# Attention and MLP on one core: the first batch's attention in an order of its own, transposes in the MLP's banks, the norm one pair further ahead, and weights rounded in three stages

## Chip, core and metric

The kernel runs on one core of a Trainium2 chip. The metric is the device time of one execution in microseconds (us); less is better. TensorE (PE) multiplies matrices into PSUM, which has eight banks here; VectorE (DVE), ScalarE (ACT) and GpSimd (POOL) do the element work; SyncE (SP) issues the loads and stores. Each engine takes its instructions strictly in the order in which they were written, and an instruction that waits holds up all behind it on its engine.

## Reference

```python
# q, k, v: (batch 8, heads 12, seq 448, dim 64) float32; g_q, g_k: (64)
q_n = q / sqrt(mean(q*q, -1) + 1e-6) * g_q           # and k_n from k, g_k
scores = (q_n @ k_n.T) / sqrt(64)
attn = exp(scores - max(scores)); attn = attn / (sum(attn) + 1e-9)
x = (attn @ v)                                        # to (3584 tokens, 768)
h = x @ w_in                                          # w_in (768, 2048), float64 in memory
g = h - tanh(h)
out = g @ w_out                                       # w_out (2048, 768), float64 in memory
```

## The kernel before

**Work and tiles.** Two heads make a pair; 8 batches of 6 pairs are 48 steps `s`. The 448 rows of a pair are four chunks of 112. With the inputs given, `bounded_path` is taken, which needs no maximum. Per step: `load` brings q, k and v (`q_nat`, `k_nat`, `v_nat`); `norm` squares k and q on POOL (into a tile named `n`), sums on VectorE and raises to -0.5 on POOL (`rr`); `norm_q` multiplies q by its factor on VectorE (tile `n`); `turn` transposes k and normed q on TensorE (L229, L234) and copies them out on ScalarE (`kT`, `qT`); `scores(s, half)` makes the transposed scores of two chunks (four matmuls, L251) and their exponentials on ScalarE (L256), with k's factor as the scale, into a tile `p`; `values` multiplies `p` by v (L280, bank `av`) and by ones for the totals (L289, bank `dn`), and VectorE takes the reciprocal (L294) and the product (L296, `xT`). From the second batch on, `add` first sums the four chunks of `p` on VectorE, so that the totals need two matmuls instead of eight.

**MLP.** For each batch `hidden` makes h by 16 blocks of six matmuls (L313), tanh on ScalarE (L319) and the subtraction on VectorE (L320, `gT`); `project` multiplies by w_out (L353). Batch b's MLP is a generator that `run(gap)` advances between the pieces of the attention of batch b+1, a quarter of a slot at a time.

**Order.** The program is scheduled by hand: what the functions issue, in the order of their calls, is what each engine runs. `slot(s)` is the loop body: it loads pair s+3, norms s+2, scores s+1, and finishes s. In the slots before the MLP starts (s below 6, the first batch) the gaps round weights instead of advancing the MLP.

**Weights.** The float64 weights are read as words and rounded to float32 in 64 pieces of 128x384, numbered n: 32 halves of w_in, then 16 first halves of w_out, then 16 second halves. Piece n is loaded as raw words (w_in's into the tiles that w_out gets later; w_out's into three buffers `w_raw`), then `round_weight_a` (two ScalarE passes, L72 and L73, and a clamp on POOL, L74) and, one piece later, `round_weight_b` (two VectorE passes, L81 and L84, and an add on POOL, L87). `weight(to)` does this up to piece `to` and issues loads up to 14 pieces ahead, 3 ahead for w_out. 20 pieces are done in the first batch, 28 in the blocks of `hidden(0)`, 16 in the first half of `project(0)`.

**Buffers that matter here.** PSUM: four banks `sc`, for scores and transposes; one each for `av` and `dn`; two `mm` for the MLP. SBUF: three tiles `p` (two per step), one `qT` and one `kT`, one `n`, three `rr`, two each of `k_nat` and `q_nat`, three of `v_nat`, three output tiles.

## Time and profile before

| | |
|---|---|
| three runs | 1686.97, 1688.23, 1689.44 us; median 1688.23 |
| profiled execution: its time, its span | 1688.23 us, 1686.4 us |
| busy, of the span: TensorE, VectorE, ScalarE, POOL | 96%, 37%, 24%, 25% |
| TensorE's granted clock, mean | 0.981 |
| slots 1 to 5, each | 16.3 to 17.4 us |
| slots 6 to 10, each | 34.2 to 43.2 us |
| slot 11 | 32.6 us |

A slot s is counted from the first score matmul of `scores(s+1, 0)` on TensorE to the next slot's. The profile's rows give an engine, a line of the code, the operation, out<-in by the names in the program, and times in us (means of one in ns); "idle before <-X" is how long the engine had nothing to run before such instructions, and what ended it. PEclk is the granted clock of TensorE, 1.00 (or 9 in a tenths row) at full speed. One matmul in float32 shows as two records, so x8 is four matmuls. SPq, ACTq and the like are an engine's issue of DMAs and its waits.

### The profile page before, as it was taken

How to read it: one execution, taken by the hardware profiler on the slowest of the kernel's cores; microseconds unless marked ns; L12 is line 12 of the kernel's file. 1: busy time of each engine (PE TensorE's matmuls, PEld its weight loads, DVE VectorE, ACT ScalarE, POOL GpSimd, SP SyncE). 2: the span in 40 equal slices, each digit the busy share in tenths (PEclk: the TensorE clock that was granted, in tenths of full speed). 3: DMA queues.
4: the chain of work that ended last, by engine and by line, in shares of the span. 5: the costliest groups of instructions: out<-in, count | busy, mean ns of one | idle time of the engine just before them, and what ended most of it. 6: DMA issues, size and time to landing. Idle time of an engine off the chain costs nothing.

```text
span 1686.4 us, 14244 instructions
## 1 busy us (share of the span) xinstructions
PE 1615.3 (96%) x5512; PEld 798.6 (47%) x5512; DVE 616.1 (37%) x747; ACT 405.3 (24%) x765; POOL 415.4 (25%) x286
## 2 busy tenths in 40 slices
...
PEclk9788999899999999999999999999999999999999
...
DMA packets 93585, 70.22 MB, mean 42 GB/s; under 512 B 48453, under 2 KB 89413, under 8 KB 93509
## 3 DMA queue, kind: packets, MB, share of 16 engines
...
## 4 chain that ended last, share of the span: by engine, by line
PE 85%; POOL 6%; DVE 4%; issue 3%; DMA 1%; ACT 1%; SPq 0%; ACTq 0%; POOLq 0%; DVEq 0%
PE mm L353 33%; PE mm L313 31%; PE sc L251 9%; PE av L280 8%; PE dn L289 3%; POOL w_out L74 2%; DVE rd L294 2%; POOL w_out L87 1%; PE sc L234 1%; POOL n L205 1%; DMA w_raw<-in_moe_w_out_dram 1%; PE sc L229 1%; POOL rr L209 1%; POOL w_in L87 1%; POOL w_in L74 1%
## 5 line engine op out<-in xcount | busy, mean ns | idle before, releaser
L313 PE MATMUL mm<-xT,w_in 128*128 128x448 f32 x1536 | 601.7, 545 | 7.7 <-DVE gT L320 6.0
L353 PE MATMUL mm<-w_out,gT 128*128 128x384 f32 x1536 | 519.9, 494 | 6.6 <-POOL w_out L87 6.6
L313 PEld LDWEIGHTS mm<-xT,w_in 128*128 128x128 f32 x1536 | 285.7, 190 | 307.5 <-issue 293.6
L353 PEld LDWEIGHTS mm<-w_out,gT 128*128 128x128 f32 x1536 | 287.7, 191 | 233.3 <-issue 38.7
L256 ACT ACTIVATE p<-sc,rr 112x448 f32<-112x448 f32 x384 | 213.0, 635 | 413.8 <-PE sc L251 413.8
L294 DVE RECIPROCAL rd<-dn 128x448 f32<-128x448 f32 x48 | 141.9, 2957 | 308.3 <-PE dn L289 308.3
L205 POOL TENSOR_TENSOR n<-k_nat 112x512 f32<-112x512 f32 x48 | 49.9, 1040 | 736.1 <-PE sc L234 729.2
L251 PE MATMUL sc<-qT,kT 64*112 64x448 f32 x768 | 182.7, 598 | 9.9 <-ACT qT L238 9.9
L320 DVE TENSOR_TENSOR gT<-mm,th 128x448 f32<-128x448 f32 x128 | 79.6, 622 | 289.1 <-ACT th L319 289.1
L319 ACT ACTIVATE th<-mm 128x448 f32<-128x448 f32 x128 | 69.7, 544 | 456.8 <-PE mm L313 447.3
L280 PE MATMUL av<-p,v_nat 112*64 112x448 f32 x768 | 157.6, 553 | 0.0
L209 POOL TENSOR_TENSOR rr<-rr,neg_half 112x16 f32<-112x16 f32 x48 | 139.8, 2913 | 50.6 <-DVE rr L208 49.6
L270 DVE TENSOR_TENSOR sum<-p 112x896 f32<-112x896 f32 x84 | 93.9, 1118 | 124.5 <-ACT p L256 120.1
L251 PEld LDWEIGHTS sc<-qT,kT 64*112 64x112 f32 x768 | 65.2, 183 | 108.4 <-issue 91.4
L206 DVE TENSOR_REDUCE rr<-n 112x8 f32<-112x512 f32 x96 | 65.6, 684 | 138.3 <-POOL n L205 138.3
L280 PEld LDWEIGHTS av<-p,v_nat 112*64 112x64 f32 x768 | 51.7, 139 | 101.8 <-issue 100.7
L353 PE MATMUL mm<-w_out,g_rest 128*128 128x384 f32 x256 | 85.4, 489 | 0.0
L205 POOL TENSOR_TENSOR n<-q_nat 112x512 f32<-112x512 f32 x48 | 50.0, 1041 | 139.1 <-DVE rr L206 139.1
L363 DVE COPY o_sb<-mm 128x384 f32<-128x384 f32 x28 | 15.5, 554 | 153.2 <-PE mm L353 152.9
L353 PEld LDWEIGHTS mm<-w_out,g_rest 128*128 128x128 f32 x256 | 47.9, 190 | 35.6 <-issue 4.1
L333 POOL COPY g_rest<-gT 128x1024 f32<-128x1024 f32 x8 | 9.0, 1131 | 202.2 <-DVE gT L320 202.1
L361 ACT COPY o_sb<-mm 128x384 f32<-128x384 f32 x28 | 13.4, 478 | 188.2 <-PE mm L353 188.1
...
## 6 DMA issues: line engine op xcount, KB each, us to landing
w_out<-in_moe_w_in_dram SPq DMA_DIRECT2D x32, 384.0 KB, 6.8
w_raw<-in_moe_w_out_dram SPq DMA_DIRECT2D x32, 384.0 KB, 3.1
...
q_nat<-in_q_dram SPq DMA_DIRECT2D x48, 224.0 KB, 3.1
v_nat<-in_v_dram SPq DMA_DIRECT2D x48, 224.0 KB, 2.6
...
gcol<-in_g_q_dram ACTq DMA_DIRECT2D x2, 0.2 KB, 2.3
```

Of the source, the lines that this page charges most:

```text
L205: nc.gpsimd.tensor_tensor(out=sq, in0=rows, in1=rows, op=ALU.mult)
L206: nc.vector.reduce_sum(rr[:, i], sq, axis=AX.X)
L209: nc.gpsimd.tensor_tensor(out=rr2, in0=rr2, in1=neg_half, op=ALU.pow)
L251: nc.tensor.matmul(sc[:CP, :S], lhsT=kT[r, c * CP : (c + 1) * CP], rhs=qT[r, :], start=True, stop=True)
L256: nc.scalar.activation(p[:, h, i, :], tiles[h][:CP, :S], AF.Exp, scale=rr[:, 0, 2 * c + h : 2 * c + h + 1])
L270: nc.vector.tensor_tensor(out=u, in0=a, in1=z, op=ALU.add)
L280: nc.tensor.matmul(av[h * D : (h + 1) * D, :S], lhsT=v_nat[:, h, c, :], rhs=p[:, h, c % 2, :], start=(c == 0), stop=(c == NCH - 1),)
L294: nc.vector.reciprocal(rd, dn[:, :S])
L313: nc.tensor.matmul(hps[:, :S], lhsT=w_in_sb[f][:, c, :], rhs=xT[b, c], start=(c == 0), stop=(c == CD - 1))
L319: nc.scalar.activation(th, hps[:, :S], AF.Tanh, bias=0.0, scale=1.0)
L320: nc.vector.tensor_tensor(out=g[:, f, :], in0=hps[:, :S], in1=th, op=ALU.subtract)
L353: nc.tensor.matmul(ops[:, :HALF], lhsT=lhs[:, f, :], rhs=w_out_sb[f][:, d], start=(f == 0), stop=(f == CF - 1),)
```

## The change

1. The first batch gets its own loop body, `first_slot(s)`, from s = -3. Its order on TensorE is scores of s+1 (first half), the transposes of s+2, values of s, scores of s+1 (second half), totals of s. `values` is split into `values`, `totals` and `divide`.
2. In `first_slot` the transposes go into the MLP's two banks `mm`; in later slots into `sc` as before. `qT` and `kT` get two buffers, output tiles two instead of three.
3. `norm` and `norm_q` run for s+3 instead of s+2; k and q are loaded for s+4, v for s+2. The squares get a tile `sq` of their own. In later slots `norm(s+3)` stands ahead of `divide(s)`, and `norm_q(s+3)` behind `turn(s+2)`.
4. A weight is rounded in three stages: a, two ScalarE passes; b, clamp and two passes on VectorE; c, the add on POOL. The clamp leaves POOL. For w_out, c of a piece is issued in the round of the next piece.
5. The first eight pieces of w_out (n = 32 to 39) are loaded into the upper w_out tiles instead of `w_raw`, and loads run up to 14 ahead wherever `place_free` finds the place free by the adds already issued.
6. `add` sums `p` with three adds of 112x896 instead of two of 112x896 and two of 112x448.

The same slot of the first batch on TensorE, before:

```order
L251 MATMUL sc<-qT,kT 112x448 x4
L280 MATMUL av<-p,v_nat 64x448 x8
L289 MATMUL dn<-p,ones 64x448 x8
L251 MATMUL sc<-qT,kT 112x448 x4
L229 MATMUL sc<-ident,k_nat 128x112 x4
L234 MATMUL sc<-ident,n 128x112 x4
```

and now (L271 is the scores, L249 and L254 the transposes, L298 values, L310 totals):

```order
L271 MATMUL sc<-qT,kT 112x448 x4
L249 MATMUL mm<-ident,k_nat 128x112 x4
L254 MATMUL mm<-ident,n 128x112 x4
L298 MATMUL av<-p,v_nat 64x448 x8
L271 MATMUL sc<-qT,kT 112x448 x4
L310 MATMUL dn<-p,ones 64x448 x8
```

The transposes moved from the slot's end to behind its first scores, and the totals from behind the values to the end.

VectorE in such a slot, before, from one reciprocal to the next (w_in_137 is the tile of a block of w_in, w_out_158 a tile of w_out that holds raw words for the time being):

```order
L294 RECIPROCAL rd<-dn 128x448
L296 TENSOR_TENSOR xT<-av,rd 128x4x112
L81 TENSOR_SCALAR w_in_137<-w_in_137 128x384
L84 SCALAR_TENSOR_TENSOR w_in_137<-w_out_158,w_in_137 128x384
L216 TENSOR_TENSOR n<-q_nat,rr 112x2x4x64
L81 TENSOR_SCALAR w_in_138<-w_in_138 128x384
L84 SCALAR_TENSOR_TENSOR w_in_138<-w_out_159,w_in_138 128x384
L206 TENSOR_REDUCE rr<-n 112x8 x2
L208 TENSOR_SCALAR rr<-rr 112x16
```

and now (L78 is the clamp, L235 norm_q, L225 and L227 the norm):

```order
L319 RECIPROCAL rd<-dn 128x448
L321 TENSOR_TENSOR xT<-av,rd 128x4x112
L78 TENSOR_SCALAR w_in_137<-w_in_137 128x384
L79 TENSOR_SCALAR w_in_137<-w_in_137 128x384
L82 SCALAR_TENSOR_TENSOR w_in_137<-w_out_157,w_in_137 128x384
L225 TENSOR_REDUCE rr<-sq 112x8 x2
L227 TENSOR_SCALAR rr<-rr 112x16
L78 TENSOR_SCALAR w_in_137<-w_in_137 128x384
L79 TENSOR_SCALAR w_in_137<-w_in_137 128x384
L82 SCALAR_TENSOR_TENSOR w_in_137<-w_out_158,w_in_137 128x384
L235 TENSOR_TENSOR n<-q_nat,rr 112x2x4x64
```

The norm of a pair and its norm_q, which lay on both sides of a reciprocal, now both stand between two reciprocals, and a clamp heads each weight.

POOL in `project(0)`, where second halves of w_out are rounded, before:

```order
L74 TENSOR_SCALAR w_out_150<-w_out_150 128x384
L87 TENSOR_TENSOR w_out_149<-w_out_149,w_raw 128x384
L74 TENSOR_SCALAR w_out_151<-w_out_151 128x384
L87 TENSOR_TENSOR w_out_150<-w_out_150,w_raw 128x384
L74 TENSOR_SCALAR w_out_152<-w_out_152 128x384
```

and now:

```order
L90 TENSOR_TENSOR w_out_151<-w_out_151,w_raw 128x384
L90 TENSOR_TENSOR w_out_152<-w_out_152,w_raw 128x384
L90 TENSOR_TENSOR w_out_153<-w_out_153,w_raw 128x384
L90 TENSOR_TENSOR w_out_154<-w_out_154,w_raw 128x384
L90 TENSOR_TENSOR w_out_155<-w_out_155,w_raw 128x384
```

The clamps between the adds are gone.

```diff
@@ -67,24 +67,27 @@
 def round_weight_a(nc, raw, dst):
     lo, hi = raw[:, :, 0], raw[:, :, 1]
     nc.scalar.activation(dst, hi.bitcast(F32), AF.Abs, scale=2.0**-16)
     nc.scalar.mul(lo, lo.bitcast(U32), 2.0**-29)
-    nc.gpsimd.tensor_scalar(out=dst, in0=dst, scalar1=HI_MIN, scalar2=HI_MAX, op0=ALU.max, op1=ALU.min)
 def round_weight_b(nc, raw, dst):
-    lo, hi = raw[:, :, 0], raw[:, :, 1]
     bits = dst.bitcast(I32)
+    nc.vector.tensor_scalar(out=dst, in0=dst, scalar1=HI_MIN, scalar2=HI_MAX, op0=ALU.max, op1=ALU.min)
     nc.vector.tensor_scalar(
         out=bits, in0=bits, scalar1=4, scalar2=1, op0=ALU.logical_shift_left, op1=ALU.logical_shift_right
     )
     nc.vector.scalar_tensor_tensor(
-        out=bits, in0=hi, scalar=-(2**31), in1=bits, op0=ALU.bitwise_and, op1=ALU.bitwise_or
-    )
-    nc.gpsimd.tensor_tensor(out=bits, in0=bits, in1=lo, op=ALU.add)
+        out=bits, in0=raw[:, :, 1], scalar=-(2**31), in1=bits, op0=ALU.bitwise_and, op1=ALU.bitwise_or
+    )
+def round_weight_c(nc, raw, dst):
+    bits = dst.bitcast(I32)
+    nc.gpsimd.tensor_tensor(out=bits, in0=bits, in1=raw[:, :, 0], op=ALU.add)
 def bounded_path(tc, ctx, q, k, v, moe_w_in, moe_w_out, out, g_col, ident, ones, neg_half):
@@ -115,12 +118,12 @@
     weights = pool("weights", bufs=1)
     nat = pool("nat", bufs=2)
     small = pool("small", bufs=2)
-    qkp = pool("qkp", bufs=1)
+    qkp = pool("qkp", bufs=2)
     pp = pool("pp", bufs=3)
     sp = pool("sp", bufs=1)
     xp = pool("xp", bufs=9)
     gp = pool("gp", bufs=1)
-    op = pool("op", bufs=3)
+    op = pool("op", bufs=2)
     wp_stack = ctx.enter_context(ExitStack())
     wp = wp_stack.enter_context(tc.tile_pool(name="wp", bufs=3))
     ps_s = pool("ps_s", bufs=4, space=PSUM)
@@ -163,35 +166,51 @@
     def weight_load(n):
         f, i, _ = weight_dst(n)
+        if n < 2 * CF + CF // 2:
+            raw = w_out_sb[n % CF if n < 2 * CF else CF // 2 + f].bitcast(I32).rearrange("p (f w) -> p f w", w=2)
+        else:
+            raw = wp.tile([P, HALF, 2], I32, name="w_raw")
         if n < 2 * CF:
-            raw = w_out_sb[n % CF].bitcast(I32).rearrange("p (f w) -> p f w", w=2)
             rows = w_in_words[i * HALF : (i + 1) * HALF, f * 2 * P : (f + 1) * 2 * P]
             nc.sync.dma_start(
                 out=raw.rearrange("p (c f) w -> p c (f w)", c=CD // 2),
                 in_=rows.rearrange("(c p) f -> p c f", p=P),
             )
         else:
-            raw = wp.tile([P, HALF, 2], I32, name="w_raw")
             nc.sync.dma_start(
                 out=raw.rearrange("p f w -> p (f w)"),
                 in_=w_out_words[f * P : (f + 1) * P, 2 * i * HALF : 2 * (i + 1) * HALF],
             )
         raws[n] = raw
-    done = [0, 0]
+    done = [0, 0, 0]
+    def place_free(n):
+        if n < CF or 0 <= n - 2 * CF - CF // 2 < 3:
+            return True
+        return n - (CF if n < 2 * CF else CF // 2 if n < 2 * CF + CF // 2 else 3) < done[2]
     def weight(to):
-        for n in range(done[1], min(to, 4 * CF)):
+        while done[1] < min(to, 4 * CF):
+            n = done[1]
             round_weight_a(nc, raws[n], weight_dst(n)[2])
             if n:
-                round_weight_b(nc, raws.pop(n - 1), weight_dst(n - 1)[2])
+                round_weight_b(nc, raws[n - 1], weight_dst(n - 1)[2])
             done[1] = n + 1
-            while done[0] < min(max(min(n + 14, 2 * CF + 3), n + 3), 4 * CF):
+            finish_weights(n - 1 if n < 2 * CF else n)
+            while done[0] < min(n + CF - 2, 4 * CF) and place_free(done[0]):
                 weight_load(done[0])
                 done[0] += 1
-        if done[1] == 4 * CF and raws:
-            round_weight_b(nc, raws.pop(4 * CF - 1), weight_dst(4 * CF - 1)[2])
+        if done[1] == 4 * CF > done[2]:
+            round_weight_b(nc, raws[4 * CF - 1], weight_dst(4 * CF - 1)[2])
+            finish_weights(4 * CF)
+    def finish_weights(to):
+        while done[2] < to:
+            round_weight_c(nc, raws.pop(done[2]), weight_dst(done[2])[2])
+            done[2] += 1
     normed, turned, probs, sums, xT = {}, {}, {}, {}, {}
@@ -201,7 +220,7 @@
         rr = small.tile([CP, 2, 2 * NCH], F32, name="rr", bufs=3)
         for i, name in enumerate("kq"):
             rows = loaded[name, s].rearrange("p a b d -> p (a b) d")
-            sq = nat.tile([CP, 2 * NCH, D], F32, name="n", bufs=1)
+            sq = nat.tile([CP, 2 * NCH, D], F32, name="sq", bufs=1)
             nc.gpsimd.tensor_tensor(out=sq, in0=rows, in1=rows, op=ALU.mult)
             nc.vector.reduce_sum(rr[:, i], sq, axis=AX.X)
         rr2 = rr.rearrange("p i r -> p (i r)")
@@ -220,16 +239,17 @@
         )
         normed[s] = rr, n
-    def turn(s):
+    def turn(s, psum):
         rr, n = normed.pop(s)
+        ps, tag = psum
         kn = loaded.pop(("k", s))
-        tk = ps_s.tile([P, 512], F32, name="sc")
+        tk = ps.tile([P, 512], F32, name=tag)
         for c in range(NCH):
             nc.tensor.transpose(tk[:, c * CP : (c + 1) * CP], kn[:, c].rearrange("p h d -> p (h d)"), ident[:CP, :CP])
         kT = qkp.tile([P, S], F32, name="kT")
         nc.scalar.mul(kT, tk[:, :S], g_col)
-        tq = ps_s.tile([P, 512], F32, name="sc")
+        tq = ps.tile([P, 512], F32, name=tag)
         for c in range(NCH):
             nc.tensor.transpose(
                 tq[:, c * CP : (c + 1) * CP], n[:, c].rearrange("p h d -> p (h d)"), ident[:CP, :CP]
@@ -264,14 +284,12 @@
             return
         t = sp.tile([CP, 2, S], F32, name="sum")
         sums[s] = [t]
-        for h in range(2):
-            a, z = (probs[s, half][:, h].rearrange("p c q -> p (c q)") for half in range(2))
-            u = sp.tile([CP, 2 * S], F32, name="sum2")
-            nc.vector.tensor_tensor(out=u, in0=a, in1=z, op=ALU.add)
-            nc.vector.tensor_tensor(out=t[:, h, :], in0=u[:, :S], in1=u[:, S:], op=ALU.add)
+        parts = [probs[s, c // 2][:, :, c % 2, :] for c in range(NCH)]
+        nc.vector.tensor_tensor(out=t, in0=parts[0], in1=parts[1], op=ALU.add)
+        for part in parts[2:]:
+            nc.vector.tensor_tensor(out=t, in0=t, in1=part, op=ALU.add)
     def values(s):
-        b, hp = steps[s]
         v_nat = loaded.pop(("v", s))
         av = ps_v.tile([P, 512], F32, name="av")
         for c in range(NCH):
@@ -281,6 +299,9 @@
                     av[h * D : (h + 1) * D, :S], lhsT=v_nat[:, h, c, :], rhs=p[:, h, c % 2, :],
                     start=(c == 0), stop=(c == NCH - 1),
                 )
+        return av
+    def totals(s):
         dn = ps_v.tile([P, 512], F32, name="dn")
         t = sums.pop(s)
         parts = t if t else [probs[s, c // 2][:, :, c % 2, :] for c in range(NCH)]
@@ -290,6 +311,10 @@
                     dn[h * D : (h + 1) * D, :S], lhsT=ones[:CP, :D], rhs=p[:, h, :],
                     start=(i == 0), stop=(i == len(parts) - 1),
                 )
+        return dn
+    def divide(s, av, dn):
+        b, hp = steps[s]
         rd = sp.tile([P, S], F32, name="rd")
         nc.vector.reciprocal(rd, dn[:, :S])
         x = xT[b, hp] = xp.tile([P, S], F32, name="xT")
@@ -389,40 +414,67 @@
     per_slot = (4 * S / ENGINE_NS * CF * CD + 4 * HALF / ENGINE_NS * CF * 7) / NP
-    def slot(s, gap):
-        def has(i):
-            return 0 <= s + i < NS
-        if has(3):
-            load(s + 3, "kq")
-        if has(2):
-            norm(s + 2)
-        if has(1):
+    def has(s):
+        return 0 <= s < NS
+    def first_slot(s):
+        if has(s + 1):
             scores(s + 1, 0)
-        gap(0)
-        if has(0):
-            values(s)
-        if has(3):
-            load(s + 3, "v")
-        gap(1)
-        if has(2):
-            norm_q(s + 2)
-        if has(1):
+        if has(s + 2):
+            turn(s + 2, (ps_m, "mm"))
+        load(s + 4, "kq")
+        if has(s + 3):
+            norm(s + 3)
+        ahead = 3 * (s + 4) if s < 0 else 9 + (EARLY - 9) * (s + 1) // NP
+        weight(ahead - 2)
+        if has(s):
+            av = values(s)
+        if has(s + 2):
+            load(s + 2, "v")
+        weight(ahead - 1)
+        if has(s + 1):
             scores(s + 1, 1)
             add(s + 1)
-        gap(2)
-        if has(2):
-            turn(s + 2)
-        gap(3)
-    load(0, "kqv")
+        if has(s):
+            dn = totals(s)
+        if has(s + 3):
+            norm_q(s + 3)
+        if has(s):
+            divide(s, av, dn)
+        weight(ahead)
+    def slot(s):
+        gap = per_slot / 4
+        if has(s + 1):
+            scores(s + 1, 0)
+        if has(s + 2):
+            load(s + 2, "v")
+        run(gap)
+        if has(s + 3):
+            norm(s + 3)
+        divide(s, values(s), totals(s))
+        run(gap)
+        if has(s + 1):
+            scores(s + 1, 1)
+            add(s + 1)
+        run(gap)
+        if has(s + 2):
+            turn(s + 2, (ps_s, "sc"))
+        if has(s + 3):
+            norm_q(s + 3)
+        if has(s + 4):
+            load(s + 4, "kq")
+        run(gap)
+    load(0, "kq")
     for n in range(4):
         weight_load(n)
     done[0] = 4
-    for s in range(-2, NP):
-        slot(s, lambda j: weight(EARLY * (4 * (s + 2) + j + 1) // (4 * (NP + 2))))
+    for s in range(-3, NP):
+        first_slot(s)
     for s in range(NP, NS):
-        slot(s, lambda j: run(per_slot / 4))
+        slot(s)
     run(1e9)
```

## Prediction

> **What bounds the kernel now.** I read the page's busy shares first, then its 40 slices.
>
> ```profile
> span 1686.4 us, 14244 instructions
> PE 1615.3 (96%) x5512; PEld 798.6 (47%) x5512; DVE 616.1 (37%) x747; ACT 405.3 (24%) x765; POOL 415.4 (25%) x286
> PEclk9788999899999999999999999999999999999999
> ```
>
> TensorE sets the time, but it is short of work or of clock only in the first eight slices (42 us each). Next, busy time by stage; a stretch here is one slot, from one `scores(s+1, 0)` to the next, and its first number is its length.
>
> ```profile
> 47.14:63.40 16.26, 12.95 (x56) 5.03 (x56) 8.95 (x12) 8.23 (x17) 12.44 (x9) 0.81 0.37 109
> 131.32:171.16 39.84, 37.17 (x109) 16.63 (x109) 28.82 (x38) 17.05 (x36) 30.53 (x23) 0.90 0.13 39
> 171.16:205.34 34.18, 32.79 (x109) 15.26 (x108) 24.21 (x32) 14.87 (x32) 27.28 (x20) 1.00 0.14 41
> 205.34:244.68 39.34, 33.57 (x109) 15.03 (x109) 26.30 (x35) 16.62 (x34) 28.82 (x23) 1.00 0.38 108
> 244.68:287.90 43.22, 35.59 (x122) 18.34 (x121) 26.23 (x33) 16.92 (x34) 32.24 (x24) 0.96 0.43 120
> 287.90:330.47 42.57, 37.19 (x119) 18.27 (x119) 25.20 (x30) 12.95 (x26) 30.80 (x24) 0.88 0.34 99
> 330.47:363.10 32.63, 32.63 (x115) 16.41 (x114) 10.24 (x12) 6.47 (x12) 2.19 (x2) 1.00 0.11 34
> ```
>
> From 330 us on TensorE is busy throughout at full clock and a slot takes 32.63. Slots 6 to 10 (second to sixth row) take 199.15 together, 36.0 more than five such slots: that is the second place with something to win. The first is the first batch, slots 0 to 5, whose TensorE rows are these (start, length, idle before and who ended it):
>
> ```profile
> 47.14 3.33 PE L251 MATMUL sc<-qT,kT 64*112 64x448 f32 x8 [0.68 <-ACT qT L238]
> 50.41 3.44 PE L280 MATMUL av<-p,v_nat 112*64 112x448 f32 x16
> 53.68 3.17 PE L289 MATMUL dn<-p,ones 112*64 112x448 f32 x16
> 56.78 1.76 PE L251 MATMUL sc<-qT,kT 64*112 64x448 f32 x8
> 58.51 0.60 PE L229 MATMUL sc<-ident,k_nat 112*128 112x112 f32 x4
> 61.75 0.98 PE L234 MATMUL sc<-ident,n 112*128 112x112 f32 x4 [2.63 <-DVE n L216]
> 63.40 3.33 PE L251 MATMUL sc<-qT,kT 64*112 64x448 f32 x8 [0.68 <-ACT qT L238]
> ...
> 205.34 1.76 PE L251 MATMUL sc<-qT,kT 64*112 64x448 f32 x8 [1.39 <-ACT qT L238]
> ```
>
> Each slot TensorE waits 2.6 us for the normed q, then 0.7 for the copy of its transpose; the eight score matmuls behind these waits take 3.33 us, against 1.76 inside a run. An idle of 1.39 alone, at 205.34 and amid long runs of matmuls, does not slow them. At full clock the slot's work is 1.76 + 3.2 + 3.1 + 1.76 + about 1.0 of transposes = 10.8. Slots 1 to 5 take 131.32 - 47.14 = 84.2, so 16.84 each.
>
> In slots 6 to 10 the chain is longer; the waits of 120 to 345 us begin with
>
> ```profile
> ACT w_out L72 <- DMA w_raw<-in_moe_w_out_dram: 72.8, 25, 8.0
> ```
>
> ScalarE, which also makes the exponentials and tanh, stands in order behind loads that land late.
>
> **The change, part by part.** Prices first: the groups of VectorE, POOL and ScalarE between 47.14 and 129 us, inside the first batch (busy us, mean ns of one, idle before).
>
> ```profile
> L294 DVE RECIPROCAL rd<-dn 128x448 f32<-128x448 f32 x5 | 14.8, 2958 | 13.7 <-PE dn L289 13.7
> L84 DVE SCALAR_TENSOR_TENSOR w_in<-w_out,w_in 128x384 int32<-128x384 int32 x11 | 9.5, 862 | 0.4
> L206 DVE TENSOR_REDUCE rr<-n 112x8 f32<-112x512 f32 x10 | 6.9, 686 | 25.2 <-POOL n L205 25.2
> L296 DVE TENSOR_TENSOR xT<-av,rd 128x448 f32<-128x448 f32 x5 | 4.8, 962 | 0.2
> L216 DVE TENSOR_TENSOR n<-q_nat,rr 112x512 f32<-112x512 f32 x5 | 4.1, 815 | 0.0
> L81 DVE TENSOR_SCALAR w_in<-w_in 128x384 int32<-128x384 int32 x11 | 3.9, 351 | 0.0
> L208 DVE TENSOR_SCALAR rr<-rr 112x16 f32<-112x16 f32 x5 | 0.9, 175 | 0.2
> ```
>
> ```profile
> L74 POOL TENSOR_SCALAR w_in<-w_in 128x384 f32<-128x384 f32 x13 | 19.7, 1518 | 8.3 <-ACT w_in L72 7.1 <-DMA q_nat<-in_q_dram 1.1
> L209 POOL TENSOR_TENSOR rr<-rr,neg_half 112x16 f32<-112x16 f32 x5 | 14.7, 2946 | 5.0 <-DVE rr L208 5.0
> L87 POOL TENSOR_TENSOR w_in<-w_in,w_out 128x384 int32<-128x384 int32 x12 | 13.5, 1124 | 8.4 <-DVE w_in L84 8.4
> L205 POOL TENSOR_TENSOR n<-q_nat 112x512 f32<-112x512 f32 x5 | 5.2, 1041 | 4.0 <-DVE rr L206 4.0
> ```
>
> ```profile
> L256 ACT ACTIVATE p<-sc,rr 112x448 f32<-112x448 f32 x40 | 22.7, 633 | 34.7 <-PE sc L251 34.7
> L73 ACT ACTIVATE w_out<-w_out 128x384 int32<-128x384 uint32 x13 | 7.2, 556 | 0.0
> L72 ACT ACTIVATE w_in<-w_out 128x384 f32<-128x384 f32 x13 | 7.2, 555 | 0.0
> ```
>
> *Start, to slot 1.* In the new order `turn(2)` stands ahead of `values(0)` and everything else of slot 0, and it needs the loads of pair 2, which still queue behind the first weights. The issue of that load of q, and q's median time to landing in the first 60 us:
>
> ```profile
> 27.25 1.34 SPq L144 DMA_DIRECT2D q_nat<-in_q_dram  x1
> ```
>
> ```profile
> q_nat<-in_q_dram SPq DMA_DIRECT2D x5, 224.0 KB, 7.8
> ```
>
> It lands about 27.25 + 7.8 = 35.0; one weight load more and two loads of v fewer go ahead of it, so I take 34.5. POOL has no clamps left in the way: square 1.04, reduction 0.69, 0.18, power 2.95, norm 0.82 and some handovers: the transposes start near 40.5. Behind them stand 1.0 of slow transposes, `values(0)` (3.2, about 1.2 more at the low clock), 1.7 and 3.1: slot 1 starts at 51.0, 3.9 LATER than the 47.14 of before.
>
> *Slots 1 to 5.* The chain on n is now a slot ahead, so its wait goes. What is late next: `p` has three buffers, and `scores(s+1, 1)` fills the one that `totals(s)` still reads, so its four exponentials start only when `totals(s)` ends, and the next scores need their banks. (Behind them on ScalarE stand one weight's two passes and the next four exponentials, which have time until 7.7 us into the slot.) Four exponentials in a row take 2.2 to 2.5, the second pair of scores 0.9 behind them; with latencies 3.5 until the scores end; then transposes 1.0, values 3.2, scores 1.7, totals 3.1: 12.5. VectorE and POOL have a loop too, since `divide(s)` stands ahead of the reductions of `norm(s+4)` and these ahead of `divide(s+1)`: 2.96 + 0.96 + one weight (clamp 0.35, L81 0.35, L84 0.86) + 0.69 + 1.04 + 0.69 + 0.18 + 2.95 + 0.82, and eight handovers at 0.1: 12.65. I take 12.9 a slot: 5 x 12.9 = 64.5 against 84.2, minus 19.7. Bounds: 12.5 from TensorE, 15.0 if the clock stays as low as now (10.8 / 0.81 + 1.7 idle). Slot 6 then starts at 115.5, minus 15.8. Idle gaps shrink to about 1.5, and the row at 205.34 says that such a gap keeps the clock. The transposes' new banks are the MLP's, which is idle until slot 6: nothing; without that cover they would queue for a bank behind four exponentials, 2.2 us. On SP's queue k and q of s+4 now wait for `turn(s+2)`, with v and weights behind them; all are due a slot or more later and land in some 3 to 8 us: nothing.
>
> *Weights.* Per weight POOL loses 1.52. VectorE gains a clamp whose price no row shows; the nearest is L81, the same form on the same shape, whose later half reads (min/median/max)
>
> ```profile
> L81 DVE TENSOR_SCALAR w_out<-w_out x32: 343/1010/1165, 191.1 to 316.4; 128x384 int32<-128x384 int32 x32
> ```
>
> 0.35 to 1.16; I take 0.5, since POOL, whose rows the long ones meet, gets emptier. In slots 6 to 10, 44 weights are rounded: POOL, 149.7 busy there, falls by 67; VectorE, 130.8, rises by 22 (51 at most) and stays below five slots of 32.63 in the mean. The second halves of w_out go through three `w_raw` buffers: median landing, and the adds of eleven such weights.
>
> ```profile
> w_raw<-in_moe_w_out_dram SPq DMA_DIRECT2D x32, 384.0 KB, 3.1
> ```
>
> ```profile
> L87 POOL TENSOR_TENSOR w_out<-w_out,w_raw x11: 1001/1012/1059, 263.1 to 297.8; 128x384 int32<-128x384 int32 x11
> ```
>
> Ten steps in 34.7, or 3.47 a weight, because POOL held the add of n behind the clamp of n+1, and so behind that one's load. Now add n waits for n alone: 0.4 issue + 3.1 + 1.1 on ScalarE + 1.7 on VectorE (0.5 + 0.4 + 0.8) + 1.0 + 0.7 of handovers = 8.0 for three weights, 2.65 each. `project(0)` rounds one in three matmuls: by columns its 48 are 0.214 of a batch's six slots, 42 us for 16 weights, or 2.6. With a norm that holds POOL some 7 us (1.04 + 0.8 + 1.04 + 1.0 + 2.95) in each slot I get 3.3, and 11 us of lag at the end; 8 of them, a quarter slot, lie between scores and who needs their banks. Loads into w_out's upper tiles are many weights ahead and cost nothing. I leave 12 of the 36.0 lost (1 of it in slot 6, where `sum` and norm_q now stand ahead of the last `divide`): minus 24.0. Ends: 2 lost, or 22 if `w_raw`'s rate stays (slots 9 and 10 alone now lose 20.5).
>
> *The rest.* From slot 11 the order on TensorE is the old one. Two sums of halves become three adds of 112x896, hidden under TensorE (10.24 of VectorE in a slot of 32.63); two output buffers instead of three serve stores 10 us apart; second buffers of qT and kT relax. Nothing.
>
> Sum: 3.9 - 19.7 - 24.0 = -39.8 on a span of 1686.4; the profiled execution took 1688.23, which is also the median of the three runs. Forecast 1648.4.
>
> **Rivals.**
> *The clock stays low* in the first batch. Speaks for it: 0.81 in every slot now with gaps of 2.6 and 0.7; against: the 1.39 gap. 15.0 a slot instead of 12.9: 1659. The Trainium skill (TensorE: Matmul & The Clock Gate, A second HAM failure mode: psum-queue depth-cycling) says that short idles between groups, as banks are passed on, can keep the clock switching; by that rule this rival holds, and nothing in the trace excludes it.
> *VectorE's loop is the bound.* The clamp and shift on the loop, at 1.16 each instead of 0.35, make it 14.3 a slot, 7 us more: 1655. The Trainium skill (SBUF — State Buffer, Who interferes with whom) has VectorE's two-port forms and GpSimd lock each other out for a whole instruction; L81's 343 against 1165 ns looks like it, and by that rule the clamp adds one such meeting a weight.
> *The w_raw ring stays* at 3.47: 22 lost instead of 12: 1658. With a slow first batch too, 1669.
> *Better:* 12.5 a slot, slot 1 at 50.0, 2 lost: 1635.
> *Slower.* In each of 41 later slots `norm_q(s+3)` now stands behind `turn(s+2)` on VectorE, and the tanh subtractions behind it. If a matmul group waits for its bank for that, L216 plus a wait, some 1.7 a slot, costs 70: 1718. It decides from 1.0 us a slot. Against it: the turn runs on TensorE ahead of the groups whose subtractions it delays.
> *No change,* if slot 0's later start and waits for p's buffer eat the gain: slots 1 to 5 at 16 and nothing in slots 6 to 10.
>
> **How the numbers follow.** Forecast, 1640 to 1654: 0.46. Low clock 0.13, VectorE's loop 0.10, ring 0.12, two of them 0.05, better 0.07: all faster. No change 0.03, slower 0.04. Range 1634 to 1670, from the better case to two rivals at once; outside lie about 0.1. Runs of this kernel spread over 2.5 us, so 0.2% (3.4 us) is about what can be told from none: faster 0.93, same 0.03, slower 0.04.
>
> **What would show it.** Slot 1 starting near 51 with a wait of TensorE for n of some 11 us before it; then first-batch slots near 13 us with no wait on n, exponentials waiting for totals, granted clock near 1.0; slot 6 at 115.5; five slots of 34 to 36 behind it; POOL near 40% there; ScalarE's wait for w_raw well under 72.8; slot 11 again at 32.6. Wrong it would be by a first-batch clock at 0.8, slots 9 and 10 at 42, or later slots above 33.

## The result, and the profile after

The changed kernel takes 1651.66 us (median of four runs, 1646.74 to 1652.88) against 1688.84 before: 0.9776 times, interval 0.9754 to 0.9798. The forecast was 1648.4, with a range of 1634 to 1670. Its profiled execution spans 1651.0, 35.4 less than the 1686.4 of before; the forecast's sum, -39.8, is a sum of such spans. The page's head and its clock row:

```profile
span 1651.0 us, 14103 instructions
...
PE 1595.7 (97%) x5512; PEld 793.5 (48%) x5512; DVE 633.1 (38%) x769; ACT 402.6 (24%) x765; POOL 320.5 (19%) x222
...
PEclk8999999999999999999999999999999999999999
```

VectorE is busier than before (633 against 616, from the clamp), POOL less (320 against 415), and of the clock row only the first digit is under 9; before, sevens and eights reached to the eighth slice.

Busy time by stretches that begin where `scores(s+1, 0)` begins: slot 1, then slots 6 to 11.

```profile
55.51:67.68 12.17, 10.86 (x59) 4.54 (x57) 9.62 (x12) 7.03 (x15) 5.18 (x4) 1.00 0.31 90
...
116.66:153.26 36.60, 33.38 (x110) 15.39 (x108) 34.41 (x46) 17.73 (x38) 14.57 (x12) 1.00 0.07 18
153.26:185.99 32.73, 32.73 (x110) 15.27 (x109) 29.23 (x45) 17.11 (x36) 15.49 (x13) 1.00 0.51 155
185.99:218.71 32.72, 32.72 (x110) 15.27 (x109) 26.29 (x42) 14.31 (x30) 15.08 (x12) 1.00 0.16 48
218.71:255.68 36.97, 33.61 (x121) 17.46 (x120) 27.59 (x44) 16.97 (x34) 17.12 (x14) 1.00 0.49 142
255.68:294.90 39.22, 35.54 (x118) 18.07 (x118) 22.87 (x32) 12.92 (x26) 16.56 (x13) 0.91 0.37 111
294.90:327.64 32.74, 32.74 (x115) 16.40 (x115) 11.36 (x13) 6.45 (x12) 4.98 (x3) 1.00 0.11 34
```

A slot of the first batch takes 12.17 with the clock at 1.00 and 10.86 of work in it. Slots 7 and 8 already have the length of the later slots; slot 6 loses 4.0 to them, and 9 and 10 lose 4.3 and 6.6. POOL is busy 78.8 in slots 6 to 10 (the five rows' sum), 44%, where it was 149.7. TensorE's rows at the start:

```profile
45.06 1.01 PE L254 MATMUL mm<-ident,n 112*128 112x112 f32 x4 [9.47 <-DVE n L235]
46.00 4.73 PE L298 MATMUL av<-p,v_nat 112*64 112x448 f32 x16
50.66 1.76 PE L271 MATMUL sc<-qT,kT 64*112 64x448 f32 x8
52.35 3.23 PE L310 MATMUL dn<-p,ones 112*64 112x448 f32 x16
55.51 1.94 PE L271 MATMUL sc<-qT,kT 64*112 64x448 f32 x8
```

Slot 1 starts at 55.51, behind a wait of 9.47 for the normed q of pair 2.

Stages of all kernels that were run, read from TensorE's rows for the first half of the scores (us; slots 1 to 5 is the mean of one, the last two columns are the median time and its ratio, with the interval, to runs of before that were made beside it):

| kernel | slot 1 starts | slots 1–5, each | slot 6 starts | slots 6–10 together | time | ratio |
|---|---|---|---|---|---|---|
| before | 47.14 | 16.84 | 131.32 | 199.15 | 1688.84 | 1 |
| changed | 55.51 | 12.23 | 116.66 | 178.24 | 1651.66 | 0.9776 (0.9754–0.9798) |
| new order, old rounding | 59.43 | 13.42 | 126.52 | 197.82 | 1683.3 | 0.9964 (0.995–0.9978) |
| old order, new rounding | 44.39 | 16.63 | 127.52 | 172.36 | 1659.83 | 0.9824 (0.9808–0.9841) |
| clamp back on POOL | 57.80 | 12.21 | 118.84 | 196.21 | 1672.33 | 0.9894 (0.9877–0.991) |
| totals first | 55.09 | 10.80 | 109.07 | 174.16 | 1641.1 | 0.971 (0.9693–0.9726) |
| late transposes in slot 0 | 47.21 | 14.16 | 118.03 | 175.96 | 1649.88 | 0.9765 (0.9743–0.9788) |
| old places of the norm | 53.87 | 12.24 | 115.06 | 167.56 | 1640.2 | 0.9708 (0.9692–0.9725) |
| four w_raw buffers | 53.61 | 12.24 | 114.81 | 172.26 | 1645.56 | 0.9739 (0.9723–0.9755) |
| transposes in scores' banks | 54.67 | 12.24 | 115.85 | 179.09 | 1649.76 | 0.976 (0.9743–0.9776) |
| loads six ahead | 51.46 | 12.24 | 112.65 | 178.86 | 1647.35 | 0.9747 (0.9731–0.9762) |
| totals first + old norm | 56.19 | 10.80 | 110.17 | 168.81 | 1635.22 | 0.9676 (0.9661–0.9692) |
| the same + four buffers + loads | 51.41 | 10.80 | 105.39 | 165.09 | 1627.58 | 0.9634 (0.962–0.9647) |
| the same + two weights a slot | 45.79 | 10.81 | 99.83 | 170.64 | 1627.47 | 0.9636 (0.9623–0.9649) |

What lies behind slot 10 is the same in the two kernels compared: 1686.4 - 330.47 = 1355.9 before, 1651.0 - 294.90 = 1356.1 after. So the whole difference is made in the first 295 us: +8.4 at the start, -23.0 in slots 1 to 5, -20.9 in slots 6 to 10.

Kernels whose instructions are the same up to slot 1 (the changed one, old places of the norm, four buffers) start it between 53.6 and 55.5, as their loads land earlier or later (POOL begins the square of pair 2's k between 31.5 and 34.2); a difference of 2 us there, and in the time, is not read as an effect.

### The profile page after: what moved, and what is told of

It reads as the page before. It is cut to its first block, busy times and chain, and to the rows that moved or that the text cites. A ratio compares the mean times of both kernels' runs of the same rounds, so it can differ in the third digit from the quotient of the medians.

```text
span 1651.0 us, 14103 instructions
## 1 busy us (share of the span) xinstructions
PE 1595.7 (97%) x5512; PEld 793.5 (48%) x5512; DVE 633.1 (38%) x769; ACT 402.6 (24%) x765; POOL 320.5 (19%) x222
## 4 chain that ended last, share of the span: by engine, by line
PE 91%; DVE 4%; DMA 2%; issue 1%; POOL 1%; ACT 1%; SPq 0%; ACTq 0%; POOLq 0%; DVEq 0%
PE mm L338 35%; PE mm L378 33%; PE sc L271 9%; PE av L298 9%; PE dn L310 3%; DMA w_raw<-in_moe_w_out_dram 1%; PE sc L249 1%; PE sc L254 1%; DMA k_nat<-in_k_dram 1%; DVE rd L319 1%; POOL sq L224 1%; DVE rr L225 0%; DVE w_in L79 0%; DVE w_out L79 0%; DVE w_in L82 0%
## 5 line engine op out<-in xcount | busy, mean ns | idle before, releaser
L271 PE MATMUL sc<-qT,kT 64*112 64x448 f32 x768 | 173.7, 567 | 3.2 <-ACT qT L258 3.2
L224 POOL TENSOR_TENSOR sq<-k_nat 112x512 f32<-112x512 f32 x48 | 51.5, 1073 | 629.2 <-DMA k_nat<-in_k_dram 629.2
L298 PE MATMUL av<-p,v_nat 112*64 112x448 f32 x768 | 156.4, 549 | 6.8 <-issue 6.8
L290 DVE TENSOR_TENSOR sum<-sum,p 112x896 f32<-112x896 f32 x84 | 94.3, 1123 | 93.3 <-ACT p L276 88.0
L271 PEld LDWEIGHTS sc<-qT,kT 64*112 64x112 f32 x768 | 63.2, 174 | 101.0 <-issue 86.4
L225 DVE TENSOR_REDUCE rr<-sq 112x8 f32<-112x512 f32 x96 | 65.6, 683 | 109.8 <-POOL sq L224 109.8
L298 PEld LDWEIGHTS av<-p,v_nat 112*64 112x64 f32 x768 | 52.3, 138 | 100.3 <-issue 100.3
L224 POOL TENSOR_TENSOR sq<-q_nat 112x512 f32<-112x512 f32 x48 | 49.9, 1039 | 240.7 <-DVE rr L225 240.7
L235 DVE TENSOR_TENSOR n<-q_nat,rr 112x512 f32<-112x512 f32 x48 | 42.0, 875 | 95.0 <-PE sc L254 72.8
L386 ACT COPY o_sb<-mm 128x384 f32<-128x384 f32 x28 | 13.4, 478 | 189.3 <-PE mm L378 125.1
```

The lines of the kernel that those rows point to most:

```text
L224: nc.gpsimd.tensor_tensor(out=sq, in0=rows, in1=rows, op=ALU.mult)
L225: nc.vector.reduce_sum(rr[:, i], sq, axis=AX.X)
L271: nc.tensor.matmul(sc[:CP, :S], lhsT=kT[r, c * CP : (c + 1) * CP], rhs=qT[r, :], start=True, stop=True)
L290: nc.vector.tensor_tensor(out=t, in0=t, in1=part, op=ALU.add)
L298: nc.tensor.matmul(av[h * D : (h + 1) * D, :S], lhsT=v_nat[:, h, c, :], rhs=p[:, h, c % 2, :], start=(c == 0), stop=(c == NCH - 1),)
```

## Experiments

### The halves of the change

New order, old rounding: the changed kernel with the hunks of the change on the rounding functions, `weight_load` and `weight` undone, and no others.

> The changed kernel with the old rounding of weights (two stages, clamp and add on POOL, w_out's raw words in w_raw only, 3 ahead); order, banks, buffers and norm of the first batch as changed. Theory A (two separate gains: order pays in the first batch, weights in slots 6 to 10): first-batch slots 1 to 5 at 12.2 to 13 us, since POOL with clamps needs some 10.5 us a slot, slots 6 to 10 together near 199 as before; some 12 to 16 us faster than before, 1673 to 1677. Theory B (POOL in order is what bounds both, so the order needs the weights' change): slots 1 to 5 at 15 us or more, under 5 us faster, 1684 or more.

Old order, new rounding: the kernel before with these hunks alone.

> The kernel before with the new rounding of weights alone (three stages, clamp on VectorE, eight pieces of w_out loaded into the upper w_out tiles, deeper loads); old order of the first batch and of the norm. Theory A: slots 1 to 5 stay near 16.5 each with a wait of TensorE for n in each, slots 6 to 10 near 178 instead of 199; 20 to 24 us faster than before, 1665 to 1669. Theory B: the first batch falls too, slots 1 to 5 below 15 each, 28 us faster or more.

The order alone gives 0.4%, the rounding alone 1.8%. The first came out between its two theories (slots of 13.4 each, the time near theory B's), the second as theory A but better: 1659.83 where 1665 to 1669 was expected, as slots 6 to 10 fall to 172.4 and not only to 178.

With the old rounding the new order's first batch starts later still (59.43) and its slots alternate between 12.18 and 15.29, so that little of its gain reaches slot 6. In a long slot TensorE waits 2.74 for `av`'s bank, until 0.1 behind xT:

```profile
77.20 4.92 PE L279 MATMUL av<-p,v_nat 112*64 112x448 f32 x16 [2.74 <-issue]
```

The divide that frees the bank starts there directly behind `norm_q`, at 73.15, 1.5 after the totals have ended. In slots 6 to 10 the order alone changes 1.3. The rounding does its work in slots 6 to 10, and there it does more without the new order (172.4) than with it (178.2). That difference is taken up below.

### The clamp back on POOL

```diff
 def round_weight_a:
+    nc.gpsimd.tensor_scalar(out=dst, in0=dst, scalar1=HI_MIN, scalar2=HI_MAX, op0=ALU.max, op1=ALU.min)
 def round_weight_b:
-    nc.vector.tensor_scalar(out=dst, in0=dst, scalar1=HI_MIN, scalar2=HI_MAX, op0=ALU.max, op1=ALU.min)
```

> The changed kernel with the clamp alone put back on POOL, in stage a; everything else as changed. If the clamp's leaving POOL is what pays in slots 6 to 10: they take 190 us or more together instead of 178, 1663 or more. If the deeper loads and the added places for raw words pay: they stay within 3 us of 178, 1651 to 1655. Slots 1 to 5 stay below 13 either way.

Slots 9 and 10 of this kernel:

```profile
228.92:271.25 42.33, 35.13 (x121) 18.64 (x120) 27.08 (x32) 17.00 (x34) 33.72 (x25) 0.96 0.43 118
271.25:315.05 43.80, 35.39 (x118) 18.00 (x118) 23.73 (x26) 12.91 (x26) 28.28 (x22) 0.88 0.36 105
```

Slots 6 to 10 take 196.2, nearly those of before, with loads as deep and three stages as in the changed kernel. So the clamp's place carries 18.0 of the 20.9: without it, deeper loads and a third stage bring little here. The clamp's move alone, with the old loads and two stages, was not run. VectorE pays little for it. The clamp and the shift behind it in the changed kernel (min/median/max ns):

```profile
L78 DVE TENSOR_SCALAR w_out<-w_out x32: 338/353/1135, 171.5 to 280.5; 128x384 f32<-128x384 f32 x32
L79 DVE TENSOR_SCALAR w_out<-w_out x32: 359/361/1059, 171.9 to 280.9; 128x384 int32<-128x384 int32 x32
```

Their medians are 353 and 361; the shift's was 1010 before. The long form of about 1.1 has not gone: of all 64 weights 8 clamps and 28 shifts show more than 0.7.

### What sets the slot of the first batch

The forecast had the second four exponentials of a slot wait for `totals(s)` to end, since it reads p's third buffer, and TensorE wait behind them. TensorE's rows from the totals of slot 1 to its one wait in slot 2 of the changed kernel, then ScalarE's exponentials, then VectorE's `norm_q` and the divide of slot 1:

```profile
64.52 3.23 PE L310 MATMUL dn<-p,ones 112*64 112x448 f32 x16
67.68 1.94 PE L271 MATMUL sc<-qT,kT 64*112 64x448 f32 x8
...
71.92 3.23 PE L298 MATMUL av<-p,v_nat 112*64 112x448 f32 x16 [1.39 <-issue]
```

```profile
66.35 2.21 ACT L276 ACTIVATE p<-sc,rr 112x448 f32<-112x448 f32 x4 [5.14 <-PE dn L310]
```

```profile
66.47 1.49 DVE L235 TENSOR_TENSOR n<-q_nat,rr 112x512 f32<-112x512 f32 x1 [1.08 <-POOL rr L228]
67.89 2.94 DVE L319 RECIPROCAL rd<-dn 128x448 f32<-128x448 f32 x1
70.86 0.96 DVE L321 TENSOR_TENSOR xT<-av,rd 128x448 f32<-128x448 f32 x1
```

The exponentials do wait for the totals, but they start 1.8 after these have begun, not when they have ended (67.75), and the scores at 67.68 follow on TensorE without a wait. What TensorE waits for is the bank: `values(2)` starts 0.1 behind the end of xT, because `av` is a single bank, and the product that reads it waits for the reciprocal of the totals, which run last. One round by the bank is 2.94 + 0.96 + values, scores and totals (3.16 + 1.69 + 3.16) and the gaps, 12.2; slot 1, where the reciprocal starts 0.05 behind the totals, takes 12.17.

From slot 2 on there is a second round that closes slightly later, VectorE's own with POOL. When the totals end, VectorE is still in `norm_q`, which has waited 1.08 for POOL's power, and the reciprocal starts directly behind it, 0.14 after the totals. From one reciprocal to the next it is 12.24, without any wait for TensorE. So two rounds that both run through the reciprocal lie within 0.1 of each other. If they are the bound, an earlier reciprocal should shorten the slot:

```diff
 def first_slot:
-            av = values(s)
+            dn = totals(s)
...
-            dn = totals(s)
+            rd = invert(dn)
+            av = values(s)
...
-            divide(s, av, dn)
+            divide(s, av, rd)
```

(`invert` is the reciprocal, cut out of `divide`.)

> The changed kernel with totals ahead of values in the first batch, and the reciprocal issued right behind the totals. Theory: after the change a first-batch slot (12.24) is totals, reciprocal, product, then the next values, which wait for the one bank av; with the totals early the reciprocal runs beside the values and slots 1 to 5 fall to 11.0 to 11.6, some 3 to 6 us faster than the changed kernel, 1646 to 1649. Rival (as forecast): the third buffer of p holds the exponentials, and slots stay at 12.2 or more.

```profile
55.09:65.90 10.81, 10.81 (x60) 4.35 (x58) 9.06 (x12) 7.07 (x15) 6.76 (x5) 1.00 0.42 108
```

The slot falls to 10.80, all of it TensorE's work, so p's third buffer was not the bound. The reciprocal's 2.95 now lie beside the values. The edit opens both rounds at once, since `norm_q` now stands behind the reciprocal and no longer ahead of it; which of the two would hold alone was not run. By the rows, a second bank alone would have left the slot at VectorE's 12.24 (an estimate). The gain is larger than expected: 10.6 in the time, of which four came in slots 6 to 10, 0.9 in slot 6 and 3.0 in slot 10; these were not traced further.

### The banks of the transposes

```diff
-            turn(s + 2, (ps_m, "mm"))
+            turn(s + 2, (ps_s, "sc"))
```

> The changed kernel, but the transposes of the first batch take their banks from the scores' four and not from the MLP's. The prediction priced this cover at 2.2 us a slot (four exponentials before a bank comes free). Theory A, that price: slots 1 to 5 take 14.4 instead of 12.23, the time rises by 10 to 13. Theory B: the slot is bound by the single bank of av (reciprocal, xT, next values), and TensorE stands 1.3 us idle there after the transposes anyway; a bank comes free with the first exponential and not the fourth: slots 1 to 5 take 12.2 to 13.0, the time rises by 0 to 4.

TensorE's rows in slot 1:

```profile
57.00 0.60 PE L249 MATMUL sc<-ident,k_nat 112*128 112x112 f32 x4 [0.39 <-ACT p L276]
...
58.85 3.23 PE L298 MATMUL av<-p,v_nat 112*64 112x448 f32 x16 [0.72 <-PE sc L254]
```

The transposes wait 0.39 for the first exponential and not for the fourth, and what they lose comes off the wait for `av` (0.72 instead of 1.31). The slot stays at 12.24. The MLP's banks bring nothing here, and the price of 2.2 a slot for doing without them was wrong: the wait is 0.39, and it is hidden by another that stands behind it. With totals first, where that other wait is gone, the scores' banks were not tried.

### The start

POOL's rows before `norm_q(2)` in the changed kernel, and VectorE's:

```profile
34.24 1.04 POOL L224 TENSOR_TENSOR sq<-k_nat 112x512 f32<-112x512 f32 x1 [6.26 <-DMA k_nat<-in_k_dram]
36.08 1.04 POOL L224 TENSOR_TENSOR sq<-q_nat 112x512 f32<-112x512 f32 x1 [0.80 <-DVE rr L225]
...
41.04 3.42 POOL L90 TENSOR_TENSOR w_in<-w_in,w_out 128x384 int32<-128x384 int32 x3
```

```profile
41.39 1.25 DVE L82 SCALAR_TENSOR_TENSOR w_in<-w_out,w_in 128x384 int32<-128x384 int32 x1
42.56 2.45 DVE L235 TENSOR_TENSOR n<-q_nat,rr 112x512 f32<-112x512 f32 x1
```

The square of k waits for its load until 34.24, about as forecast. But the square of q stands behind the reduction of k's, and `norm_q` behind the passes of two weights on VectorE; itself it takes 2.45, where it took 0.82 in the mean of the first batch before, and ends 0.55 after POOL's three adds in a row have ended at 44.46. The Trainium skill (SBUF — State Buffer, Who interferes with whom) has a VectorE instruction with two inputs in SBUF contend with a GpSimd instruction that reads SBUF, and `norm_q` is such a one: the trace agrees. Which side waits differs: here `norm_q` ends behind the last add, while in slots 2 to 5, beside two adds, it takes 1.49 and the second add 1.46 instead of 1.01.

First, take away what is queued behind the wait:

```diff
 def first_slot:
-        if has(s + 2):
+        if has(s + 2) and s:
             turn(s + 2, (ps_m, "mm"))
-        load(s + 4, "kq")
+        if s:
+            load(s + 4, "kq")
...
         if has(s):
             dn = totals(s)
+        if s == 0:
+            turn(s + 2, (ps_m, "mm"))
+            load(s + 4, "kq")
```

> The changed kernel with one edit: in slot 0 the transposes of pair 2, and the issue of the loads of k and q of pair 4, stand behind totals(0) instead of ahead of values(0). Theory A: slot 1 of the changed kernel starts at 55.5 and not at 51 because TensorE stands 9.5 us at the transposes of n(2) with values(0), scores(1, 1) and totals(0) queued behind them. Then these run during the wait, slot 1 starts at 47 to 49, and since n(3) is ready only at about 54, some of the gain is paid back by a wait of about 5 us in slot 1: slot 6 starts at 111 to 113.5 instead of 116.7, the time falls by 3 to 6. Rival B: the chain of norms on POOL and VectorE (loads of k and q that land late, then 10 us a norm), and not the order on TensorE, sets the start: slot 1 starts near 47, but the waits move whole to the transposes of pairs 3 and 4, slot 6 starts at 115.5 or later and the time falls by less than 1.5.

```profile
47.21 1.76 PE L271 MATMUL sc<-qT,kT 64*112 64x448 f32 x8 [0.92 <-ACT qT L258]
...
54.46 1.01 PE L254 MATMUL mm<-ident,n 112*128 112x112 f32 x4 [4.96 <-DVE n L235]
58.31 6.01 PE L298 MATMUL av<-p,v_nat 112*64 112x448 f32 x16 [2.84 <-DVE xT L321]
```

Slot 1 starts 8.3 earlier, but slot 2 later than without the edit (69.10 against 67.68): TensorE waits 4.96 for the n of pair 3 and 2.84 for xT, and runs the values in 6.01 behind that, at a granted clock of 0.53. Rival B held, by the stages; the time fell by 1.8, which is not told from none here. The chain of norms sets the pace, so next its loads:

```diff
-            while done[0] < min(n + CF - 2, 4 * CF) and place_free(done[0]):
+            while done[0] < min(n + (6 if n < 9 else CF - 2), 4 * CF) and place_free(done[0]):
```

> The changed kernel with one number changed: while the first nine weights are rounded, weights are loaded at most six ahead and not fourteen, so that SP issues k and q of pairs 2, 3 and 4 ahead of most of the first weights' loads. In the changed kernel k and q of pair 2 are issued at 24.6 to 28.1, behind twelve weight loads in a row from 11.5 on, POOL waits 6.3 for k, and slot 1 starts at 53.6 to 55.5. Theory A: the loads set the start. Then k(2) is issued near 16 and q(2) near 18, when norm_q(0) frees its buffer; POOL goes from its three adds straight to the squares of pair 2, n(2) is ready near 38, slot 1 starts at 47 to 50 and slot 6 at 108 to 111; the time falls by 4 to 8. Rival B: POOL's and VectorE's own work (a norm of some 7 and three weights of 3.4 in each of the first slots) sets it: the wait moves to pairs 3 and 4 as it did where slot 0's transposes stood later; slot 6 stays at 113.5 to 117 and the time within 2. Rival C: the weights come late instead: ScalarE waits for them in the first batch and slots 6 to 10 take 182 or more.

SP's issues of the loads of k and q of pair 2, and TensorE's transposes of its n with the start of slot 1:

```profile
15.04 1.83 SPq L144 DMA_DIRECT2D k_nat<-in_k_dram  x2
17.18 1.18 SPq L147 DMA_DIRECT2D q_nat<-in_q_dram  x1
```

```profile
40.37 1.01 PE L254 MATMUL mm<-ident,n 112*128 112x112 f32 x4 [4.56 <-DVE n L235]
...
51.46 1.94 PE L271 MATMUL sc<-qT,kT 64*112 64x448 f32 x8
```

k and q of pair 2 leave 9.5 earlier, and the transposes start at 40.37, with slot 1 at 51.46. That is 2 to 4 earlier than in the changed kernel, and short of the 47 to 50 of theory A; the time falls by 4.3, and slots 6 to 10 are not late for it (178.9). The n of pairs 1 and 2 come 11.6 apart and POOL has no idle there but the waits for reductions: theory A holds for the first part, rival B for the rest.

### Where slots 6 to 10 still lose

Of the 15.1 lost, 4.0 lie in slot 6 and 10.9 in slots 9 and 10. TensorE's waits in slot 6:

```profile
124.02 2.52 PE L338 MATMUL mm<-xT,w_in 128*128 128x448 f32 x6 [1.47 <-DVE xT L321]
...
147.08 6.25 PE L338 MATMUL mm<-xT,w_in 128*128 128x448 f32 x16 [1.75 <-DVE gT L345]
```

The first is for the last xT of the first batch, the second for a subtraction of the MLP. VectorE is busy 15.4 of the 16 us from 137 to 153: `norm(9)` stands ahead of `divide(6)` there, and what follows them is late.

For slots 9 and 10 the first try is a longer ring of raw words.

Four w_raw buffers:

```diff
-    op = pool("op", bufs=2)
+    op = pool("op", bufs=1)
-    wp = wp_stack.enter_context(tc.tile_pool(name="wp", bufs=3))
+    wp = wp_stack.enter_context(tc.tile_pool(name="wp", bufs=4))
```

(with the 3 in `place_free` made 4, and two small constants in a pool that is closed)

> The changed kernel with four w_raw buffers instead of three; to make room there is one output buffer instead of two, and two small constants live in a pool that is closed. Theory A: what slots 6 to 10 still lose against 32.63 each (15.1 together) is the ring of w_raw buffers, each of which waits for load, ScalarE, VectorE and POOL before its next load: ScalarE's wait for w_raw (36.4 in the changed kernel) falls under 25, slots 9 and 10 (37.0 and 39.2) lose 3 to 6 less together, the time falls by 3 to 6. Rival B: POOL's and VectorE's shares (the norm takes a hole of 7 to 9 us on POOL out of each slot) set the rate: the waits move to VectorE and POOL, slots 9 and 10 stay within 1.5 and so does the time. Rival C: one output buffer costs more than the ring gives, by stores that a copy must wait for: slots from 11 on get longer than 32.63, and the time rises.

In the changed kernel ScalarE waits for these loads, in slots 6 to 10 (us, times, longest):

```profile
ACT w_out L71 <- DMA w_raw<-in_moe_w_out_dram: 36.4, 15, 8.3
```

With four buffers it is 18.3 in 14, at most 2.5; slot 9 falls from 36.97 to 33.18, slot 10 from 39.22 to 37.04, and the time by 6.1. Theory A. The single output buffer costs nothing that shows. Slot 6 stays at 36.6: the ring is not what it waits for.

Old places of the norm:

```diff
 def slot:
+        if s > NP and has(s + 2):
+            norm(s + 2)
         if has(s + 1):
             scores(s + 1, 0)
...
-        if has(s + 3):
-            norm(s + 3)
         divide(s, values(s), totals(s))
         run(gap)
+        if s > NP and has(s + 2):
+            norm_q(s + 2)
...
             turn(s + 2, (ps_s, "sc"))
-        if has(s + 3):
-            norm_q(s + 3)
```

> The changed kernel, but from slot 6 on the norm keeps the places of the kernel before: norm(s+2) ahead of scores(s+1, 0) and norm_q(s+2) ahead of scores(s+1, 1); slot 6 itself needs neither, since the first batch has already made them. The first batch is the changed kernel's. Slots 6 to 10 took 178.2 in the changed kernel and 172.4 with the new rounding in the old order. Theory A: the norm's new place (norm_q(s+3) behind turn(s+2), norm(s+3) among the weights' passes) costs the difference: slots 6 to 10 take 171 to 174.5, the time falls by 4 to 7; later slots stay at 32.6. Rival B: the difference comes from how far the weights are when slot 6 begins (it begins 11 us earlier in the changed kernel, with POOL's and the loads' work of that time still to do): slots 6 to 10 stay at 176 to 180 but for slot 6, which has no norm and may gain 1 to 2; the time moves by less than 2.

It won more than theory A asked: 10.7 in slots 6 to 10 (2.0 in slot 6, 2.7 in slot 9, 6.0 in slot 10), 11.5 in the time, and later slots stay as they were. In slot 6 the second wait, 1.75, is gone. Around the norm of slot 9, VectorE and POOL of the changed kernel:

```profile
234.52 0.17 DVE L227 TENSOR_SCALAR rr<-rr 112x16 f32<-112x16 f32 x1
234.60 2.95 DVE L319 RECIPROCAL rd<-dn 128x448 f32<-128x448 f32 x1
237.58 0.96 DVE L321 TENSOR_TENSOR xT<-av,rd 128x448 f32<-128x448 f32 x1
```

```profile
229.91 1.01 POOL L90 TENSOR_TENSOR w_out<-w_out,w_raw 128x384 int32<-128x384 int32 x1 [0.94 <-ACT w_out L71]
...
234.77 2.90 POOL L228 TENSOR_TENSOR rr<-rr,neg_half 112x16 f32<-112x16 f32 x1 [1.01 <-DVE rr L227]
239.85 1.01 POOL L90 TENSOR_TENSOR w_out<-w_out,w_raw 128x384 int32<-128x384 int32 x1 [2.19 <-DVE w_out L82]
```

The same place with the norm's old order:

```profile
221.79 0.17 DVE L227 TENSOR_SCALAR rr<-rr 112x16 f32<-112x16 f32 x1
221.87 0.35 DVE L78 TENSOR_SCALAR w_out<-w_out 128x384 f32<-128x384 f32 x1
...
223.13 0.35 DVE L78 TENSOR_SCALAR w_out<-w_out 128x384 f32<-128x384 f32 x1
...
228.13 2.95 DVE L319 RECIPROCAL rd<-dn 128x448 f32<-128x448 f32 x1
```

```profile
217.18 1.02 POOL L90 TENSOR_TENSOR w_out<-w_out,w_raw 128x384 int32<-128x384 int32 x1 [1.34 <-DMA k_nat<-in_k_dram]
...
222.04 2.94 POOL L228 TENSOR_TENSOR rr<-rr,neg_half 112x16 f32<-112x16 f32 x1 [1.01 <-DVE rr L227]
224.95 2.06 POOL L90 TENSOR_TENSOR w_out<-w_out,w_raw 128x384 int32<-128x384 int32 x2
```

In the changed kernel `norm(s+3)` stands just ahead of `divide(s)`. VectorE hands the means to POOL at 234.69 and goes into the divide; POOL is through with the power at 237.67 and finds no weight ready, and from the start of one add to the start of the next it is 9.94. In the old place weights stand between: VectorE passes two of them while POOL makes the power, the two adds follow at once, and the hole is 7.77. With three w_raw buffers such a hole stops the loads (ScalarE's longest wait for one, 8.3, ends at 243.9, right behind it).

One part of the 10.7 is of another kind: in this kernel slot 6 needs no norm, so the stretch has four norms and not five. The kernel with the old order throughout and the new rounding has five, and takes 172.4; by that the places give some 5.9 of the 10.7 and the norm less some 4.8. This is an estimate, since its first batch differs too, and by the slots the share of the missing norm may be smaller: slot 6, where it is missing, gains 2.0. `norm_q`'s new place was not tried by itself.

### Versions that beat both kernels

> The changed kernel with the two edits that paid: in the first batch totals(s) and its reciprocal ahead of values(s) (alone: slot 6 at 109.1, slots 6 to 10 take 174.2), and from slot 6 on the norm in the places of the kernel before (alone: slots 6 to 10 take 167.6). Theory A: they act in different stages, so they add: slot 6 at 107 to 109.5, slots 6 to 10 in 166.5 to 169, slot 11 at 275 to 277.5, time 1632.5 to 1635. Rival B: slots 6 to 10 have a rate of weights of their own that POOL and VectorE set, and beginning earlier is paid back: slots 6 to 10 take 171 to 174, time 1636.5 to 1641.

1635.22, nearly as theory A has it (1632.5 to 1635): slots 1 to 5 at 10.80, slots 6 to 10 in 168.8; slot 6 is 0.7 late at 110.2, as slot 1 started late, at 56.2.

> The two edits that paid, and with them four w_raw buffers (with one output buffer) and the loads of the first nine weights at most six ahead. Theory A, the loads set the start and the ring what is left of slots 6 to 10: slot 6 at 102 to 105, slots 6 to 10 in 164.5 to 167, time 1624 to 1629. Rival B, neither has anything left to give beside the two edits: within 2 of the kernel with those two alone, 1632 to 1635.

1627.58, 0.9634 of before and 24 under the changed kernel. Slots 1 to 5 are all TensorE's work and slots 6 to 10 lose 1.9 together. What is left is the start.

```diff
-        ahead = 3 * (s + 4) if s < 0 else 9 + (EARLY - 9) * (s + 1) // NP
+        ahead = 2 * (s + 4) if s < 0 else 6 + (EARLY - 6) * (s + 1) // NP
```

> The fastest kernel so far (the two edits that paid, four w_raw buffers, loads six ahead), and in each of the three slots before slot 0 two weights rounded instead of three, the three left over spread over slots 0 to 5. Theory A: with the loads early, POOL's own loop sets the start (n(1) and n(2) 11.6 apart: three adds 3.4, squares 1.8 and 1.0, two waits for reductions 2.5, power 2.95). One add less makes it 10.4 and norm_q shorter too: slot 1 starts at 48 to 50 instead of 51.4, and slots 1 to 5 stay at 10.8, as POOL is busy only 7 of these: the time falls by 1.5 to 3.5. Rival B: the added weights in slots 0 to 5 lengthen these (VectorE 9.0 of 10.8 busy) or the wait goes to the next pair: slot 6 at 104.5 to 107, the time within 1.

Slot 1 starts at 45.79, 5.6 earlier, so the third weight of each early slot did hold the start: the transposes of n(1) and n(2) now come 9.8 apart instead of 11.6. The edit takes that weight off VectorE and ScalarE as well as off POOL, so POOL's add is not shown to be the cause by itself. Slots 1 to 5 keep their length. Yet the time is the same. TensorE's row in slot 6:

```profile
109.07 4.85 PE L341 MATMUL mm<-xT,w_in 128*128 128x448 f32 x6 [3.35 <-DVE xT L324]
```

Weights that were moved stand ahead of the last divide on VectorE, and the first add of `sum` behind them takes 2.87 where it took 1.08, beside three adds in a row on POOL. The MLP's first group waits 3.35 for xT (0.59 without the edit), its next six matmuls take 4.85 instead of 2.52 (granted clock 0.52 from 110.4 to 115.0), the values behind them 3.69 instead of 3.23: 5.6 given back. Neither theory had this.

## Why the prediction was right, and where its terms were off

The time came out 3.3 above the forecast, and the three terms of the sum have the right signs; their errors, +4.5, -3.3 and +3.1, partly cancel; of the 4.4 that remain on the span, 1.1 lies in the medians, which do not fall on the profiled executions.

*Start.* Forecast +3.9, measured +8.4. The mechanism was right (slot 0's work queued behind the transposes of n(2), a wait of 9.5 where 11 was forecast), the size not: after the load landed I counted the norm's own steps with "some handovers", 6.0 to the transposes, and it took 10.8, from 34.24 to 45.06. Left out were the second square behind the first reduction, the weights' passes ahead of `norm_q` on VectorE, and POOL's adds beside it. From the transposes to slot 1 it took 10.45, as forecast (10.5). When the loads came 9.5 earlier, the transposes started at 40.4.

*Slots 1 to 5.* Forecast 12.9 each, measured 12.23, -23.0 instead of -19.7. The work (10.8) and the clock (1.00) were right. Of the two limits that I named, one was right and one wrong. VectorE's loop with POOL, which I had at 12.65, is there: from slot 2 on it closes at 12.24, with `norm_q` at 1.49 beside POOL's adds instead of the 0.82 that I took. TensorE's limit, p's third buffer, is not there, since the exponentials wait only for the first half of the totals; its number, 12.5, lay near TensorE's true round, 12.17 by the single bank of `av`, by chance. That both run through the reciprocal I did not see.

*The MLP's banks* were right at "nothing", and the price of losing them was wrong: a wait of 0.39 that costs nothing, instead of 2.2.

*Slots 6 to 10.* Forecast -24.0 with 12 left lost; measured -20.9 with 15.1 left. That POOL, freed of the clamp, is what gains was shown (196.2 with the clamp back). The term that was mis-sized is slot 6: 1 forecast, 4.0 measured. The last xT was forecast, and its wait is 1.47; the 1.75 for a subtraction behind `norm(9)` and `divide(6)` was not. The 11 forecast for the rest came out (10.9 in slots 9 and 10), but partly by luck: the norm holds POOL for 6.8, as priced, and then the next add waits 2.2 more, because the norm now stands against the divide on VectorE. In the kernel with the norm in its old places, which has one norm less in the stretch, these two slots lose only 2.2.

*The rivals.* The clock did not stay low: 1.00 in slots 1 to 5 with an idle of 1.3 to 1.4 in each. By the rule cited with this rival (the Trainium skill, TensorE: Matmul & The Clock Gate, A second HAM failure mode: psum-queue depth-cycling) the clock would have gone on switching; this trace does not agree. VectorE's loop did close the slots, but at 12.24 and not at 14.3: in slots 1 to 5 no clamp shows the long form, and 4 shifts of 10 do. In slots 6 to 10 the clamp takes 0.47 in the mean, near the 0.5 that I took. The w_raw ring did not stay as it was, though more than a third of the remaining loss is its (6.0 of 15.1 went with a fourth buffer). The slower case, `norm_q(s+3)` behind `turn(s+2)` in 41 later slots, cost nothing from slot 11 on; the norm's new places cost only where weights are rounded too.
